# One core: w_in and w_out products of a fused mLSTM cell and gated feed-forward as concurrent 64-row pairs from the third chunk on

## The chip, the cores and the metric

The kernel runs on one core of a Trainium2 chip. A core has a matrix engine (TensorE, PE in the profile, with its weight loads shown as PEld), a vector engine (VectorE, DVE), an activation engine (ScalarE, ACT), a general engine (GpSimd, POOL) and a queue engine (SyncE, SP), which here issues transfers (DMAs). Each engine takes its own instructions in order and waits on semaphores that the others raise. TensorE multiplies a stationary operand that lies on up to 128 rows (partitions) with a moving operand and adds the result up in a bank of PSUM, a memory of eight banks of 128 partitions x 512 float32; VectorE and ScalarE read it from there.

The metric is the device time of one execution in microseconds: the median over runs.

## The reference

Inputs are q, k, v of shape (4, 8, 768, 40), input, forget and output gates, and the weights w_in (320 x 2048) and w_out (2048 x 320). Cut to what matters:

```python
for t in range(S):                                  # mLSTM cell, per batch b and head h
    m_new = np.maximum(f_gate[:, :, t] + m, i_gate[:, :, t])
    f_stab = np.exp(f_gate[:, :, t] + m - m_new)
    i_stab = np.exp(i_gate[:, :, t] - m_new)
    m = m_new
    C = f_stab[:, :, None, None] * C + i_stab[:, :, None, None] * np.einsum('bhd,bhe->bhde', vt, kt)
    n = f_stab[:, :, None] * n + i_stab[:, :, None] * kt
    h_tilde = np.einsum('bhde,bhe->bhd', C, qt)
    denom = np.maximum(np.abs(np.einsum('bhd,bhd->bh', n, qt)[:, :, None]), 1.0)
    y[:, :, t] = sigmoid(o_gate[:, :, t]) * h_tilde / denom
x = y.transpose(0, 2, 1, 3).reshape(3072, 320)      # B*S tokens, H*D features
h = x @ w_in
out = (h * np.cos(h)) @ w_out
```

All of it is float32.

## The kernel before

**Chunks and cells.** The sequence of 768 steps is cut into six chunks of 128 (`NC` = 6). A cell is one chunk of one batch entry, numbered n = c * 4 + b. A cell has within-chunk scores (`scores`, L475: 40 rows, the two heads of a pair on rows 0 to 39 and 64 to 103), decays (`decay_exponents`, `decay`), weighted scores (`weigh`, L481, VectorE), values (`values`, L501 to L510: the tile `vt`, made of pieces of 32 columns of the array), the update of the recurrent state (`seam`, L601: the tile `pu`, 40 columns; `state`, L627, VectorE) and the normalisation (`normalize_turned`, L521 to L538, VectorE), which writes the transposed tokens `xT`, and through `low_out` their last 64 features `xL`.

**The feed-forward.** x has 320 features: `NK` = 2 blocks of 128 rows and a rest of 64. `both_parts(c, b)` takes a chunk's tokens (512 over the four batch entries) through two of eight stages f2 while the cells of the next chunk run. A stage is one `Up`: two tiles `pup` of 128 x 512, one for each block of 128 hidden features, in two PSUM banks (`ps_u`). Each gets two matmuls over 128 rows (L650) and one over 64 rows (L644); the 64-row matmuls of the two tiles use rows 0 to 63 and rows 64 to 127. In even stages and in the last chunk the 64-row pair comes last, in odd ones first. Then ScalarE rounds (`near`, L658), VectorE takes the rest (`rest`, L661), ScalarE takes the sine (`sin`, L666), VectorE multiplies (`gate`, L670). The next stage's `pup` tiles are free once the gates have read them.

**The second product.** From the second chunk on w_out is applied by a scheme with fewer products. `sums` (L719 to L727, VectorE and GpSimd) makes sums and differences S and D of the gated tiles, and `products` gives twelve matmuls of 128 rows and 160 columns per stage (fourteen in the last chunk) into four banks, `acc` = X0, X1, Y0, Y1 (pool `ps_o`, four banks). Sixteen `late_products` per chunk take two more sums into a tile `late` in one bank of the same pool. `combine_first` (L772, ScalarE), `combine` (L780 to L790, VectorE) and `combine_late` (L795 to L797) add the banks up into output tiles, which `out_to` (L696) stores. L760 is the matmul of all these products.

**What sets the order.** It is written out by hand (a manual schedule): each engine gets its instructions in the order of the calls, with semaphores where data pass. `down_slot(c, f2)` says which products are issued at the end of a stage: at f2 = 0 the last twelve of the chunk before, at f2 = 1 the sixteen late ones and then `combine_late`, from f2 = 2 on an even share of this chunk's. `combine` of the chunk before is issued in stage 0, behind the normalisation of that stage's cell. The transfers of q, k, v, decays (`load_E`, tiles E and G), output gates (`load_o`) and the stores are issued on SP where they stand in the code.

The two matmuls of a stage, and the slot of stage 1:

```python
for e, pu in enumerate(self.pu):
    r = slice(64 * e, 64 * e + 64)
    nc.tensor.matmul(pu, w_in_l[r, f2], xL[c][r].rearrange("p b t -> p (b t)"), start=ahead, stop=not ahead)
...
if f2 == 1 and c > 1:
    run(late_products(c - 1), NF)
    combine_late(c - 1)
    return
```

## Time and profile before

| | us |
|---|---|
| median of three runs | 534.6 (534.35 to 534.88) |
| the profiled execution | 531.87, of which the span from the first to the last instruction is 530.1 |
| TensorE busy in the span | 512.8 (97%) |
| VectorE busy | 406.9 (77%) |
| ScalarE busy | 286.6 (54%) |
| GpSimd busy | 247.9 (47%) |

The mean granted clock of TensorE is 0.988. The page gives busy times by engine; a group line names a source line, an engine, the tiles written and read, the shape and how often (x), then busy time and mean duration, then the idle time of the engine ahead of them and what ended it. A float32 matmul shows as two records, two passes. Matmuls overlap, so the time of one is read from start to start, not from its duration. A timeline line has the start and the length in us, the engine, the line, the operation, the tiles and the shape; merged lines are several instructions in a row. SPq is the queue engine's own work, such as issuing a transfer.

Where the chunks lie, by the timeline: the first stage of c = 2 starts at 210.1, of c = 3 at 290.2, of c = 4 at 370.2, of c = 5 at 448.8.

### The profile page before, as it was taken

The page shows a single profiled execution, that of the slowest core. Times are in us where ns is not written, and L with a number is a line of the kernel's source. Part 1 is how long each engine was busy: PE and PEld are TensorE (multiplying, and loading weights), DVE is VectorE, ACT ScalarE, POOL GpSimd, SP SyncE. Part 2 cuts the span into 40 slices and gives each one's busy share as a digit, 9 for nine tenths or more (in the row PEclk, how much of TensorE's full clock was granted, in tenths as well). Part 3 has the DMA queues.
Part 4 walks back from the last instruction along what each step waited for, and adds up shares of the span by engine and source line. Part 5 has one row for each costly group of instructions (what it writes and reads, how often), then busy time and mean ns, then how long its engine had stood idle before and what let it go on. Part 6 is the DMA issues. An engine that isn't in the chain of part 4 may idle for free.

```text
span 530.1 us, 10427 instructions
## 1 busy us (share of the span) xinstructions
PE 512.8 (97%) x3848; PEld 346.9 (65%) x3848; DVE 406.9 (77%) x828; ACT 286.6 (54%) x546; POOL 247.9 (47%) x409
## 2 busy tenths in 40 slices
PE   7999779999999999999999999999999999999996
PEld 3875354556657666676677677677667676666765
DVE  4896798997778878888778888868898878664636
ACT  2896797857556537744547635537735531312221
POOL 7536454673775684554454554453433333121211
PEclk9999879999999999999999999999999999999999
DMA  9999999999339259149159149159110000000001
GB/s 139 227 183 213 231 195 231 246 238 208 48 118 196 56 109 181 41 120 170 56 116 157 42 113 176 49 116 160 47 56 6 1 6 6 26 25 1 1 0 50
DMA packets 97762, 57.81 MB, mean 109 GB/s; under 512 B 62048, under 2 KB 89792, under 8 KB 97712
## 3 DMA queue, kind: packets, MB, share of 16 engines
q1 hardware_dynamic: 96240, 55.64, 51.1%
q0 software_dynamic: 1424, 1.49, 1.4%
q8 instruction: 30, 0.49, 0.4%
q14 instruction: 20, 0.16, 0.1%
q10 hardware_dynamic: 48, 0.02, 0.0%
HBM read 51.71 MB, written 4.11 MB: 105 GB/s over the span
## 4 chain that ended last, share of the span: by engine, by line
PE 81%; DVE 7%; DMA 6%; POOL 1%; issue 1%; SPq 1%; ACT 1%; DVEq 0%; POOLq 0%
PE pup L650 26%; PE acc L760 25%; PE pup L644 8%; PE ps L475 4%; PE po L682 3%; PE late L760 3%; DMA bits<-in_moe_w_in_dram 3%; PE vt L510 2%; PE vt L501 2%; PE pu L601 2%; DMA o<-in_o_gate_dram 1%; PE pw L832 1%; DVE t L456 1%; PE ph L491 1%; DMA bits<-in_moe_w_out_dram 1%
## 5 line engine op out<-in xcount | busy, mean ns | idle before, releaser
L650 PE MATMUL pup<-xT,w_in_sb 128*128 128x512 f32 x384 | 176.7, 603 | 3.1 <-DVE g L670 2.9
L658 ACT ACTIVATE n<-pup 128x512 int32<-128x512 f32 x96 | 54.0, 595 | 193.6 <-PE pup L644 141.6
L650 PEld LDWEIGHTS pup<-xT,w_in_sb 128*128 128x128 f32 x384 | 70.4, 191 | 90.3 <-issue 88.0
L661 DVE SCALAR_TENSOR_TENSOR n<-pup,n 128x512 f32<-128x512 f32 x96 | 63.0, 687 | 82.3 <-ACT n L658 80.9
L724 POOL TENSOR_TENSOR D<-g 128x128 f32<-128x128 f32 x40 | 19.7, 492 | 145.6 <-DVE g L670 145.6
L666 ACT ACTIVATE n<-n 128x512 f32<-128x512 f32 x96 | 59.3, 631 | 16.1 <-DVE n L661 16.1
L670 DVE SCALAR_TENSOR_TENSOR g<-pup,n 128x512 f32<-128x512 f32 x96 | 61.9, 684 | 2.2 <-ACT n L666 1.4
L760 PE MATMUL acc<-w_out_sb,g 128*128 128x160 f32 x320 | 58.6, 304 | 0.0
L760 PE MATMUL acc<-T,g 128*128 128x160 f32 x320 | 58.0, 301 | 0.1
L644 PE MATMUL pup<-xL,w_in_l 64*128 64x512 f32 x192 | 55.2, 650 | 0.9 <-POOL w_in_l L162 0.9
L607 POOL DMA_DIRECT2D xL<-xT x40 | 22.5, 563 | 65.1 <-DVE xT L538 61.6
L760 PEld LDWEIGHTS acc<-w_out_sb,g 128*128 128x128 f32 x320 | 47.8, 190 | 5.6 <-issue 4.2
L760 PEld LDWEIGHTS acc<-T,g 128*128 128x128 f32 x320 | 48.1, 190 | 3.7 <-issue 3.0
L406 ACT ACTIVATE E<-E,tab 128x128 f32<-128x128 f32 x160 | 49.0, 389 | 0.2
L682 PE MATMUL po<-w_out_sb,g 128*128 128x320 f32 x128 | 36.2, 436 | 0.0
L760 PE MATMUL acc<-T,S 128*128 128x160 f32 x160 | 35.0, 300 | 0.0
L475 PEld LDWEIGHTS ps<-t,t 40*128 40x128 f32 (+1 forms) x384 | 24.2, 187 | 12.6 <-DVE t L456 7.5
L682 PEld LDWEIGHTS po<-w_out_sb,g 128*128 128x128 f32 x128 | 24.0, 190 | 11.9 <-issue 1.9
L481 DVE TENSOR_TENSOR E<-ps,E 128x512 f32<-128x512 f32 x48 | 30.7, 680 | 1.4 <-PE ps L475 1.3
L644 PEld LDWEIGHTS pup<-xL,w_in_l 64*128 64x128 f32 x192 | 14.8, 187 | 24.0 <-issue 19.6
L760 PE MATMUL acc<-w_out_sb,S 128*128 128x160 f32 x160 | 28.8, 299 | 0.0
L962 ACT ACT_TABLE_LOAD x22 | 28.2, 1283 | 0.4
(178 smaller groups left out, 878.0 us busy)
## 6 DMA issues: line engine op xcount, KB each, us to landing
E<-M_d SPq DMA_DIRECT2D x22, 512.0 KB, 4.3
qr<-in_q_dram SPq DMA_DIRECT2D x36, 160.0 KB, 3.1
kr<-in_k_dram SPq DMA_DIRECT2D x36, 160.0 KB, 5.4
G<-G_d SPq DMA_DIRECT2D x20, 256.0 KB, 5.2
bits<-in_moe_w_out_dram SPq DMA_DIRECT2D x8, 640.0 KB, 5.8
bits<-in_moe_w_in_dram SPq DMA_DIRECT2D x16, 256.0 KB, 7.6
out_dram<-o_sb SPq DMA_DIRECT2D x24, 160.0 KB, 1.9
ks<-in_k_dram SPq DMA_DIRECT2D x10, 320.0 KB, 7.5
```

What stands on the lines that cost most here:

```text
L406: nc.scalar.activation(out=Es[n][:, h], in_=Es[n][:, h], func=AF.Exp, scale=-1.0, bias=tab[:, c, 0, g:g + 1])
L475: nc.tensor.matmul(ps[j][:, p], kT[r, p], qT[r, p], start=True, stop=True)
L481: nc.vector.tensor_tensor(out=w, in0=pss[n][j], in1=w, op=OP.mult)
L644: nc.tensor.matmul(pu, w_in_l[r, f2], xL[c][r].rearrange("p b t -> p (b t)"), start=ahead, stop=not ahead)
L650: nc.tensor.matmul(pu.rearrange("p (b t) -> p b t", b=B), w_in_sb[:, i, ts(2 * f2 + e, 128)], xT[c][:, i:NK * B:NK], start=(i == 0 and not ...
L658: nc.scalar.activation(out=self.n[e], in_=self.pu[e], func=AF.Copy, bias=0.25)
L661: nc.vector.scalar_tensor_tensor(out=self.n[e].bitcast(FP), in0=self.pu[e], scalar=0.25, in1=self.n[e], op0=OP.add, op1=OP.subtract)
L666: nc.scalar.activation(out=r, in_=r, func=AF.Sin, scale=TWO_PI_DOWN)
L670: nc.vector.scalar_tensor_tensor(out=g, in0=self.pu[e], scalar=TWO_PI, in1=self.n[e].bitcast(FP), op0=OP.mult, op1=OP.mult)
L682: nc.tensor.matmul(po[c][b], gs[c, f][:, ts(b, C)], w_out_sb[:, f], start=(f == 0), stop=(f == NF - 1))
L760: nc.tensor.matmul(a, lhs, rhs, start=start, stop=stop)
L962: nc.scalar.activation(out=spot, in_=spot, func=AF.Sin)
```

## The change

From the third chunk on (c >= 2) every w_in and w_out product is split into its lower and upper 64 rows, and the two halves of different products run as a pair side by side, each writing a bank of its own. `Up.split` takes the two `pup` tiles through five pairs: in the first two, rows 0 to 63 write the second tile and rows 64 to 127 the first; then the tiles are exchanged for three more. `steps` does the same for the w_out products: the upper half runs six products (eight in the last chunk) ahead of the lower, so that the halves are on different banks. `both` issues a pair. When a bank passes from one half to the other, SP waits for the first half's last matmul and signals TensorE (a `nop` on SP), and the first matmul of the other half waits for that signal. Between the two parts of a stage `apart` puts two or three w_out steps, in stage 1 two of the late ones.

The late products have two banks of `ps_o` instead of one. `UPTO` says how many w_out products of a chunk are issued by the end of each stage, in place of equal shares. In the last chunk every third `pup` tile lies in one of the banks of the scores' pool (`thirds`), and that pool's two banks are given out by name (`Banks`). The matmuls of `pu` are cut into 32 and 8 columns in all cells. Half of `state` moves behind the gates of odd stages.

Transfers go through a list: until c = 1 they are issued at once, from c = 2 on up to four are issued between the two parts of each stage and up to two behind `seam`. In the diff, `load_o`, `load_two` and `out_to` change in the same way as `load_E`: `nc.sync.dma_start` becomes `transfer`.

```diff
     dram = ctx.enter_context(tc.tile_pool(name="dram", bufs=1, space=bass.MemoryType.DRAM))
-    ps_a = ctx.enter_context(tc.tile_pool(name="ps_a", bufs=2, space=bass.MemoryType.PSUM))
+    class Banks:
+        def __init__(self, name, tags):
+            self.pool, self.tags, self.turn = ctx.enter_context(tc.tile_pool(name=name, bufs=1, space=bass.MemoryType.PSUM)), tags, 0
+        def tile(self, shape, dtype, name, tag):
+            self.turn = (self.turn + 1) % len(self.tags)
+            return self.pool.tile(shape, dtype, name=name, tag=self.tags[self.turn])
+    ps_a = Banks("ps_a", ("a0", "a1"))
     ps_u = ctx.enter_context(tc.tile_pool(name="ps_u", bufs=2, space=bass.MemoryType.PSUM))
...
+    todo, at_once = [], [True]
+    def transfer(out, in_):
+        todo.append((out, in_))
+        if at_once[0]:
+            issue(len(todo))
+    def issue(n):
+        for _ in range(min(n, len(todo))):
+            dst, src = todo.pop(0)
+            nc.sync.dma_start(out=dst, in_=src)
     def load_o(c, bs=range(B)):
...
-            nc.sync.dma_start(out=E, in_=M_d[1][(c - 1) * BH + b * H:(c - 1) * BH + (b + 1) * H].unsqueeze(0).to_broadcast([128, H, C]))
+            transfer(out=E, in_=M_d[1][(c - 1) * BH + b * H:(c - 1) * BH + (b + 1) * H].unsqueeze(0).to_broadcast([128, H, C]))
...
                     h = 2 * p + j
-                    nc.tensor.matmul(pu[64 * j:64 * j + D, p], kws[n][:, h, 0:D], vs(n)[:, h], start=True, stop=True)
+                    for lo, hi in ((0, 32), (32, D)):
+                        nc.tensor.matmul(pu[64 * j + lo:64 * j + hi, p], kws[n][:, h, lo:hi], vs(n)[:, h], start=True, stop=True)
             pus[n] = pu
...
-    def state(n):
+    def state(n, part=slice(0, 4)):
         if n < N - B:
-            for j, r, s, w in halves(n):
+            for j, r, s, w in list(halves(n))[part]:
                 u = increment(n, r, w)
...
+    SYNC = mybir.DependencyInfo(mybir.DependencyClass.Sync, mybir.DependencyReason.DATA)
+    over = []
+    class Bank:
+        def __init__(self, tile):
+            self.tile, self.half, self.seen = tile, None, None
+    def both(low, high, done):
+        passed = max(bank.seen if bank.half == 1 - half else 0 for half, bank, *_ in (low, high))
+        for half, bank, a, lhs, rhs, start, stop in (low, high):
+            r = slice(64 * half, 64 * half + 64)
+            ins = nc.tensor.matmul(a, lhs[r], rhs[r], start=start, stop=stop).ins
+            if passed:
+                tc.add_manual_dep(ins, over[passed - 1].name, SYNC, reason="a bank passes from one half to the other")
+            bank.half, bank.seen = half, len(over) + 1
+        if done:
+            over.append(nc.sync.nop().ins)
+            tc.add_manual_dep(over[-1], ins.name, SYNC, reason="the halves are done with their banks")
+    thirds = {2 + 6 * i + x for i in range(3) for x in (0, 3)}
+    def third(shape, dtype, name, tag):
+        return ps_a.pool.tile(shape, dtype, name=name, tag=ps_a.tags[spare_bank])
+    spare_bank = 1
     class Up:
...
             self.c, self.f2 = c, f2
-            self.pu = [ps_u.tile([128, B * C], FP, name="pup", tag="up") for _ in range(2)]
+            self.pu = [(third if c == NC - 1 and 2 * f2 + e in thirds else ps_u.tile)([128, B * C], FP, name="pup", tag="up") for e in range(2)]
+            (self.split if c > 1 else self.whole)(c, f2)
+            self.n = [p3.tile([128, B * C], I32, name="n", tag="n") for _ in range(2)]
+        def split(self, c, f2):
+            banks = [Bank(pu) for pu in self.pu]
+            def product(half, e, i, start=False):
+                pu = self.pu[e]
+                if i < NK:
+                    return (half, banks[e], pu.rearrange("p (b t) -> p b t", b=B), w_in_sb[:, i, ts(2 * f2 + e, 128)],
+                            xT[c][:, i:NK * B:NK], start, False)
+                return half, banks[e], pu, w_in_l[:, f2], xL[c].rearrange("p b t -> p (b t)"), False, True
+            for i in range(NK):
+                both(product(0, 1, i, i == 0), product(1, 0, i, i == 0), i == NK - 1)
+            apart(c, f2)
+            issue(4)
+            for i in range(NK + 1):
+                both(product(0, 0, i), product(1, 1, i), False)
+        def whole(self, c, f2):
...
                 low()
-            self.n = [p3.tile([128, B * C], I32, name="n", tag="n") for _ in range(2)]
...
         made = [(X0, 0, G0[:, 0, 0], B11), (X0, 1, G1[:, 0, 0], B21), (X0, 2, S[:, 0], T2),
-                (Y0, 0, G0[:, 0, 1], T3), (Y0, 1, G1[:, 0, 1], T4), (Y0, 2, S[:, 2], T1),
-                (Y1, 2, S[:, 3], B22),
-                (X1, 0, G0[:, 1, 0], B11), (X1, 1, G1[:, 1, 0], B21), (X1, 2, S[:, 1], T2),
-                (Y1, 0, G0[:, 1, 1], T3), (Y1, 1, G1[:, 1, 1], T4)]
+                (Y0, 1, G1[:, 0, 1], T4), (Y0, 0, G0[:, 0, 1], T3), (Y0, 2, S[:, 2], T1)]
         if c == NC - 1:
-            L = late[c]
-            made += [(L, 0, D1, T1), (L, 1, D4, B22)]
-        banks = [id(t) for t, *_ in made]
-        for j, (t, i, lhs, rhs) in enumerate(made):
-            yield t[:, i], lhs, rhs, k == 0 and id(t) not in banks[:j], k == LAST and id(t) not in banks[j + 1:]
+            made += [(late[c], 0, D1, T1), (late[c], 1, D4, B22)]
+        made += [(X1, 0, G0[:, 1, 0], B11), (X1, 1, G1[:, 1, 0], B21), (X1, 2, S[:, 1], T2),
+                 (Y1, 1, G1[:, 1, 1], T4), (Y1, 0, G0[:, 1, 1], T3), (Y1, 2, S[:, 3], B22)]
+        made = [(bank, bank.tile[:, i], lhs, rhs) for bank, i, lhs, rhs in made]
+        if c == 1 and k < LAST:
+            banks = [bank for bank, *_ in made]
+            for j, (_, a, lhs, rhs) in enumerate(made):
+                yield a, lhs, rhs, k == 0 and banks[j] not in banks[:j]
+        else:
+            yield from steps(made, len(made) - 6, k == 0, k == LAST)
+    def steps(made, ahead, first, last):
+        n = len(made)
+        issued = [(half, *made[k]) for j in range(n) for half, k in enumerate((j, (j + ahead) % n))]
+        banks = [m[1] for m in issued]
+        for x in range(0, 2 * n, 2):
+            yield *((*issued[y], first and banks[y] not in banks[:y], last and banks[y] not in banks[y + 1:]) for y in (x, x + 1)), \
+                banks[x:x + 2] != banks[x + 2:x + 4]
     def late_products(c):
-        L = late[c] = ps_o.tile([128, 2, HALF], FP, name="late", tag="o")
-        for k in range(NF // 2):
-            for i, rhs in ((0, wv[:, k, 0, 1]), (1, wv[:, k, 1, 1])):
-                yield L[:, i], Ds[c][:, k, i], rhs, k == 0 and i == 0, k == LAST and i == 1
+        L = late[c] = [Bank(ps_o.tile([128, HALF], FP, name="late", tag="o")) for _ in range(2)]
+        made = [(L[e], L[e].tile, Ds[c][:, k, e], wv[:, k, e, 1]) for e in range(2) for k in range(NF // 2)]
+        return steps(made, NF // 2, True, True)
...
         for _ in range(n):
-            a, lhs, rhs, start, stop = next(made)
-            nc.tensor.matmul(a, lhs, rhs, start=start, stop=stop)
+            now = next(made)
+            if len(now) == 3:
+                both(*now)
+            else:
+                a, lhs, rhs, start = now
+                nc.tensor.matmul(a, lhs, rhs, start=start, stop=False)
     def all_products(c):
-        acc[c] = [ps_o.tile([128, 3, HALF], FP, name="acc", tag="o") for _ in range(4)]
+        acc[c] = [Bank(ps_o.tile([128, 3, HALF], FP, name="acc", tag="o")) for _ in range(4)]
         if c == NC - 1:
-            late[c] = ps_a.tile([128, 2, HALF], FP, name="late", tag="a")
+            late[c] = Bank(ps_a.pool.tile([128, 2, HALF], FP, name="late", tag=ps_a.tags[1 - spare_bank]))
         for k in range(NF // 2):
...
         o = outs_of[c, p] = [out_tile() for _ in range(2)]
-        nc.scalar.copy(out=o[1][:, 0:HALF], in_=acc[c][p][:, 0])
+        nc.scalar.copy(out=o[1][:, 0:HALF], in_=acc[c][p].tile[:, 0])
...
-        X0, X1, Y0, Y1 = acc[c]
+        X0, X1, Y0, Y1 = (bank.tile for bank in acc[c])
         X, Y = (X0, Y0) if p == 0 else (X1, Y1)
...
         o, L = outs_of[c, 1], late[c]
-        tt(out=o[0][:, HALF:DM], in0=L[:, 0], in1=o[0][:, HALF:DM], op=OP.add)
-        tt(out=o[1][:, HALF:DM], in0=L[:, 0], in1=o[1][:, HALF:DM], op=OP.add)
-        tt(out=o[0][:, HALF:DM], in0=L[:, 1], in1=o[0][:, HALF:DM], op=OP.add)
+        L0, L1 = (L.tile[:, 0], L.tile[:, 1]) if c == NC - 1 else (L[0].tile, L[1].tile)
+        tt(out=o[0][:, HALF:DM], in0=L0, in1=o[0][:, HALF:DM], op=OP.add)
+        tt(out=o[1][:, HALF:DM], in0=L0, in1=o[1][:, HALF:DM], op=OP.add)
+        tt(out=o[0][:, HALF:DM], in0=L1, in1=o[0][:, HALF:DM], op=OP.add)
         for e in range(2):
...
-    made_of = {}
+    made_of, late_of = {}, {}
+    done = [0] * NC
+    UPTO = [None, [12 * f2 for f2 in range(8)]] + [[0, 3, 13, 30, 40, 57, 67, 84]] * (NC - 3) + [[0, 3, 19, 35, 51, 67, 83, 98]]
+    def run_to(c, n):
+        if c not in made_of:
+            made_of[c] = all_products(c)
+        run(made_of[c], n - done[c])
+        done[c] = n
+    def apart(c, f2):
+        if f2 == 1 and c > 1:
+            late_of[c - 1] = late_products(c - 1)
+            run(late_of[c - 1], 2)
+        else:
+            d = c if f2 else c - 1
+            run_to(d, done[d] + (2 if c == NC - 1 or f2 % 2 else 3))
...
             else:
-                run(made_of[c - 1], 12)
+                run_to(c - 1, 12 * (LAST + 1))
             return
         if f2 == 1 and c > 1:
-            run(late_products(c - 1), NF)
+            run(late_of[c - 1], LAST - 1)
+            run_to(c, UPTO[c][f2])
+            run(late_of[c - 1], LAST + 1)
             combine_late(c - 1)
             return
-        if c not in made_of:
-            made_of[c] = all_products(c)
-        each = 14 if c == NC - 1 else 12
-        quota = [0] * 8
-        for m in range(2, 8):
-            quota[m] = each * 7 * (m - 1) // 6 - each * 7 * (m - 2) // 6
-        run(made_of[c], each if c == 1 else quota[f2])
+        run_to(c, UPTO[c][f2])
...
                 if cell:
-                    state(n)
+                    state(n, slice(0, 2))
                 for e in range(2):
...
                     up.gate(e)
+                if cell:
+                    state(n, slice(2, 4))
                 if c > 0:
...
                 seam(n)
+                issue(2)
                 normalize_turned(n)
...
         for c in range(NC):
+            at_once[0] = c < 2
             for b in range(B):
                 both_parts(c, b)
-        run(made_of[NC - 1], 14)
+        issue(len(todo))
+        at_once[0] = True
+        run_to(NC - 1, 14 * (LAST + 1))
         for p in range(2):
...
         for p in range(2):
```

More of the change, by code (lines that the diff above doesn't have):

```diff
@@ L309, in load_o @@
                 dst = raw_o[c][32 * a:32 * a + 32].rearrange("t b (g k) d -> t g b (k d)", g=2)[:, g]
-                nc.sync.dma_start(out=dst, in_=src[a, g, c])
+                transfer(out=dst, in_=src[a, g, c])
     def sigmoid(c, bs=slice(0, B)):
@@ L339, in load_two @@
                         dst = raws[name][m][64 * j + 32 * low:64 * j + 32 * low + 32, x:x + WR]
-                        nc.sync.dma_start(out=dst.rearrange("t (p x) -> t p x", x=C // 32 * D),
-                                          in_=src[j, c, :, 4 * b:4 * b + 8])
+                        transfer(out=dst.rearrange("t (p x) -> t p x", x=C // 32 * D), in_=src[j, c, :, 4 * b:4 * b + 8])
         for name, dst, src in (("K", ks2[m], k), ("v", vs2[m], v)):
@@ L344, in load_two @@
                 src = src.rearrange("b h (c t) d -> c t b h d", t=C)
-                nc.sync.dma_start(out=dst[:, :, :, 0:D], in_=src[c, :, b:b + 2])
+                transfer(out=dst[:, :, :, 0:D], in_=src[c, :, b:b + 2])
     def load_E(n):
@@ L360, in load_E @@
             for j in range(2):
-                nc.sync.dma_start(out=G[64 * j:64 * j + 64], in_=src[j, HP * b:HP * b + 2 * HP].unsqueeze(0).to_broadcast([64, 2 * HP, C]))
+                transfer(out=G[64 * j:64 * j + 64], in_=src[j, HP * b:HP * b + 2 * HP].unsqueeze(0).to_broadcast([64, 2 * HP, C]))
             Gs[n], Gs[n + 1] = G[:, 0:HP], G[:, HP:2 * HP]
@@ L695, in out_to @@
     def out_to(c, b, o):
-        nc.sync.dma_start(out=out[b * S + c * C:b * S + (c + 1) * C], in_=o)
+        transfer(out=out[b * S + c * C:b * S + (c + 1) * C], in_=o)
     def weight_sums(part):
```

## The prediction

> **What bounds the kernel now.** I read the page's busy shares first, then the chain that ended last, then the waits, and last the timelines of TensorE, VectorE and SyncE in one chunk. Chunks are numbered c = 0 to 5, as in the code; "stage f2" is one of the eight w_in steps of a chunk.
>
> The page, busy times and the chain's shares:
>
> ```profile
> PE 512.8 (97%) x3848; PEld 346.9 (65%) x3848; DVE 406.9 (77%) x828; ACT 286.6 (54%) x546; POOL 247.9 (47%) x409
> ...
> PE 81%; DVE 7%; DMA 6%; POOL 1%; issue 1%; SPq 1%; ACT 1%; DVEq 0%; POOLq 0%
> ```
>
> TensorE is the bound, and the waits leave it little idle time:
>
> ```profile
> PE pup L650 <- DVE g L670: 2.9, 1, 2.9
> PE vt L501 <- DVE E L481: 2.8, 1, 2.8
> ```
>
> Each is one wait, early in the run. So from c = 2 on only TensorE's own work, and new waits, count. The chain in order of time (start, length, what; a float32 matmul is two records, x8 are four matmuls):
>
> ```profile
> 242.85 3.63 PE pup L650 x8
> 246.48 3.80 PE acc L760 x28
> 250.28 3.43 PE pup L650 x8
> 253.72 1.06 PE pup L644 x4
> 255.67 4.00 PE acc L760 x28
> ```
>
> The same work costs 0.20 us more behind a change of the array's shape: 3.63 against 3.43, 4.00 against 3.80. L644 is the 64-row pair; two pairs of passes at 0.429 (3.43/8) would be 0.86, and 1.06 is again 0.20 more. So a switch costs 0.20, and a 512-column pass costs 0.429 as full rows or as a pair. A 160-column pass costs 3.80/28 = 0.136, a w_out product 0.272.
>
> TensorE's timeline behind the first stage of c = 3 (start, length, line, shapes):
>
> ```profile
> 294.64 1.06 PE L475 MATMUL ps<-t,t 40*128 40x128 f32 x16
> 295.63 0.81 PE L760 MATMUL acc<-w_out_sb,g 128*128 128x160 f32 x4
> ...
> 299.09 0.42 PE L501 MATMUL vt<-E,vs 128*32 128x128 f32 x8
> ...
> 300.75 0.54 PE L601 MATMUL pu<-vs,kw 128*40 128x48 f32 x16
> 301.22 1.13 PE L644 MATMUL pup<-xL,w_in_l 64*128 64x512 f32 x4
> 302.28 3.70 PE L650 MATMUL pup<-xT,w_in_sb 128*128 128x512 f32 x8
> 305.82 4.51 PE L760 MATMUL late<-w_out_sb,D 128*128 128x160 f32 x32
> ```
>
> VectorE in the same stretch:
>
> ```profile
> 300.40 0.28 DVE L722 TENSOR_TENSOR g<-g 128x128 f32<-128x128 f32 x1
> 300.89 0.32 DVE L521 STREAM_TRANSPOSE dt<-vt 128x128 f32<-128x128 f32 x1 [0.21 <-PE vt L510]
> ...
> 303.95 0.48 DVE L780 TENSOR_TENSOR o_sb<-acc,o_sb 128x320 f32<-128x320 f32 x1
> ...
> 305.24 0.31 DVE L784 TENSOR_TENSOR o_sb<-acc,o_sb 128x160 f32<-128x160 f32 x1
> ```
>
> VectorE works through gates, sums, normalisation and the combination of the previous chunk's banks almost without a gap; L784 ends at 305.55, only 0.27 before `late` starts. That near coincidence carries the forecast.
>
> **The change part by part.**
>
> *Switches removed.* A period of two stages with a cell (20.02 us, 241.72 to 261.74) has six shape changes: full to pair, pair to full twice, full to 32 columns (vt), vt to pu, pu to pair. Afterwards two stay, into vt and out of pu. Three at 0.20 go, and vt to pu, 0.14 (0.11 as vt's last step to pu is 0.20 against 0.09 inside vt, and 0.03 in pu's first step). In c = 2 and 3: 8 periods x 0.74. In c = 4 there is no pu: 4 x 0.60 = 2.4. In c = 5 each stage loses two: 8 x 0.40 = 3.2. The number of 512-column slots stays, five per stage.
>
> *pu in 32-column pieces.* 16 records become 32. Bounds: no dearer (its eight steps of 0.042 run four column tiles at once), or 32 x 0.030, vt's mean of 1.66/56, so 0 to 0.6 per cell. Four tiles side by side start 7 ns apart in vt, so I take 0.06. The 8 periods above then give 5.4; the 8 earlier cells in the loop (c = 0 and 1) give 0.08 x 8 = 0.6; the four first cells gain a switch each between px and pu, 0 to 0.8 as TensorE waits there anyway, taken as 0.3. Sum of all this: -11.3.
>
> *The pairs' own pace.* Against 0.136, the scores' pairs cost 0.111 for 128 columns, where streaming as L760 does would give 0.109. So 0 to 0.0024 per pass, on some 950 passes: 0 to 2.3, and 0.5 taken, since the 512-column pairs showed no excess. [...]
>
> *Signals through SP.* 172 wait-and-signal instructions. A matmul's end reaches SP in 0.07 (E's load behind the last vt), VectorE's end reaches TensorE in 0.09; with an SP wait of 0.03 a hand-over takes about 0.2. A 512-column pass ends 0.59 after its start; the other half wants its weights 0.84 after it when two products lie between, so 0.25 of room. For products (end 0.30, use 0.82) it is 0.5. So nothing, as long as SP is free.
>
> *Transfers.* Four issues behind the first half of each stage, two behind pu. At 0.45 to 0.6 each, four take 2 us, and the second half of the stage covers 2.57. The exception, SP's timeline:
>
> ```profile
> 242.78 0.59 SPq L345 DMA_DIRECT2D ks<-in_k_dram  x1
> 243.46 3.83 SPq L345 DMA_DIRECT2D vs<-in_v_dram  x1
> ```
>
> In stage 5 of c = 2 and 3 the batch is G, ks, vs, E. TensorE needs the next signal some 4.1 after the batch begins. SP is through after 2.0 if vs issues freely, and after 7.5 with vs at 4.0 and an E behind it at 2.2 (the one at 78.15). So 0 to 3.4 twice; E and a G leave some 4 us earlier than now, so the backlog before vs is smaller: 0.4 each, 0.8.
>
> *The late products, earlier and in two banks.* Today `late` starts behind a whole stage 1 and takes one bank. Now two of its steps stand between the halves of stage 1, low half and high half in a bank each. By the waits in the changed program these are the banks of X0 and Y0, so TensorE waits for the fourth combination (L784), and the stage's second half, the remaining late products and all that follows queue behind that wait in order. Counted from the end of stage 0 (294.64): VectorE is through after 10.91, less the 0.21 it waited for vt, which now comes sooner; plus 0.09, 10.79. TensorE arrives after scores 0.89, nine products 2.45 (three went between the halves before), switch 0.10, vt 1.55, pu 0.40, switch 0.20 and four passes 1.72: 7.31. It stands 3.5. So in c = 2 too (L784 10.9 behind the stage there); 3.9 in c = 4 without pu. In c = 5 no normalisation precedes: stage 0 ends at 453.31, L784 at 460.73, release 7.51. TensorE needs 2.72 for ten products, waits for the first gate (456.35, so 3.13), and arrives at 4.85: 2.7 plus 0.4. Together 14.0.
>
> *What is late next.* Stage 2 puts products between its halves whose banks the late combination frees: sums and L795 to L797 end about 0.3 behind TensorE's arrival in c = 2 to 4, 0.2 in c = 5: 1.1. With seven instead of fourteen products ahead of vt in even stages, the second weighting (3.3 behind the stage's end, plus 0.1) is 0.1 late, nine times: 0.9. The shorter gaps still cover the gates: 4.9 in even stages against 4.6, 4.07 in odd ones against 3.9 (half of the state update moved behind the gates, and the pair end costs the head start of the first bank). The third bank in c = 5 needs only one gate, 3.13 against 3.80.
>
> **Sum:** -11.3 + 14.0 + 0.5 + 0.8 + 1.1 + 0.9 = +6.0. The profiled execution took 531.87 (span 530.1 and 1.8 around it), which would become 537.9; the median of the runs, 534.6, is 2.7 above it and becomes **540.6**.
>
> **The rivals.**
> - *SP behind vs.* Both batches cost 3.4 instead of 0.4: 546.6. For it: vs at 2.8 to 4.0 in every row. Against: E and two G right ahead of it there.
> - *Faster: the wait doesn't bite.* If the fourth combination were through before TensorE arrives (7.3 behind stage 0, against 10.8 by the rows), the 14.0 go: 526.6. It decides at about 2.0 us of standing per chunk: below that the kernel is faster. Against it: VectorE has only 0.21 of idle time to give.
> - *Hand-overs slower than 0.25.* 0.1 on each of 172 is 17 more: 558. For it: no row shows a signal through SP. Against: each of its legs has a row.
> - *No concurrency.* Pairs one after the other would double TensorE's time from 215 on, some 300 us more: 840. Against: the scores' pairs start 7 ns apart.
> - *Pairs quicker than full rows.* If part of the 0.136 were the load, pairs would come down to the columns' share of a 512-column pass, 0.429 x 160/512 = 0.134: 950 x 0.002 and the 0.5 not spent, 538.2. Against: loads of 190 ns already run under full passes of 0.136. [...]
>
> **How the numbers follow.** Chances: forecast 0.60, SP behind vs 0.15, faster 0.13, slow hand-overs 0.07, no concurrency 0.02, quicker pairs 0.03. Low end 535: all small terms at zero (537.3, without the 3.3), and 2.3 for an error of a sixth in the 14.0. High end 549: pairs at 2.3 and SP at 6.8 add 7.8 to the forecast. The forecast alone spans 535 to 545. 0.2% (1.1 us) is about what a measurement of this kernel can tell from no change. Of the 0.60, 0.05 lie within 1.1 of 534.6 and 0.03 below, so faster 0.16, same 0.05, slower 0.79.
>
> **What would show it.** Right: TensorE idle some 3.5 us ahead of `late` in c = 2 to 4 and 2.7 in c = 5, ended by VectorE; 512-column pairs at 0.43, 160-column ones at 0.136 to 0.139; vt to pu without a step; span near 536. Wrong: no such idle time (faster), idle time ended by SP in stage 5 or at every bank change (slower), or pair steps longer than these.

## The result, and the profile after

The changed kernel is slower: 548.3 us, the median of four runs (545.9 to 551.2), against 534.5 for the kernel before on the same chip (four runs, 532.9 to 534.9). The ratio is 1.0271, 95% interval 1.0236 to 1.0306. The forecast was 540.6 in a range from 535 to 549: the direction was right and the median lies just within the range, but the 6.0 us forecast became 13.8.

The profiled execution after took 550.01 (span 548.2). Its page, busy times and the clock that was granted to TensorE, in tenths, over 40 slices of 13.7 us:

```profile
PE 510.7 (93%) x5376; PEld 377.7 (69%) x5376; DVE 406.8 (74%) x828; ACT 285.2 (52%) x546; POOL 247.5 (45%) x409
...
PEclk9999989999999999899989999989979999999999
```

TensorE is busy about as long as before (512.8) in a span 18.1 us longer. The row of the clock has dips in slices 17, 21, 27 and 30, between 219 and 411 us, where the pairs run. A slice is too coarse to see what they are. First the waits, TensorE from 215 us to its last product (who waited for whom: us in total, times, longest):

```profile
PE late L667 <- DVE o_sb L863: 8.2, 4, 2.5
PE acc L667 <- SPq L672: 3.7, 2, 1.9
PE late L667 <- DVE o_sb L867: 2.4, 4, 0.7
PE acc L667 <- DVE S L790: 0.5, 1, 0.5
```

The kernel before stands 0.3 us in all from c = 2 on; this one stands 15.2 (two waits of 0.2 are left out above). Most of it is the wait that the prediction put into stage 1, in c = 2 on the timeline (start, length, line):

```profile
220.61 1.99 PE L667 MATMUL pup<-xT,w_in_sb 64*128 64x512 f32 x8
...
224.26 0.48 DVE L863 TENSOR_TENSOR o_sb<-acc,o_sb 128x320 f32<-128x320 f32 x1
...
224.80 0.54 PE L667 MATMUL late<-w_out_sb,D 64*128 64x160 f32 x2 [2.20 <-DVE o_sb L863]
...
225.54 0.31 DVE L867 TENSOR_TENSOR o_sb<-acc,o_sb 128x160 f32<-128x160 f32 x1
...
226.00 1.13 PE L667 MATMUL late<-w_out_sb,D 64*128 64x160 f32 x5 [0.67 <-DVE o_sb L867]
```

TensorE is through with the first part of the stage at 222.6, stands 2.20 for the first combination, runs the first late product and stands 0.67 more for the fourth (L784 of the kernel before is L867 here). The other wait is SP's, in stage 5 of c = 2:

```profile
267.46 0.45 SPq L319 DMA_DIRECT2D G<-G_d  x1
267.96 0.74 SPq L319 DMA_DIRECT2D ks<-in_k_dram  x1
268.80 2.01 SPq L319 DMA_DIRECT2D vs<-in_v_dram  x1
...
270.57 0.71 PE L667 MATMUL acc<-T,g 64*128 64x160 f32 x8
271.00 2.32 SPq L319 DMA_DIRECT2D E<-M_d  x1
...
273.42 1.32 PE L667 MATMUL acc<-w_out_sb,g 64*128 64x160 f32 x8 [1.87 <-SPq L672]
...
275.06 1.28 PE L667 MATMUL acc<-T,g 64*128 64x160 f32 x8
```

SP issues vs in 2.0 and the E behind it in 2.3, and the signal that a bank is free stands behind both; c = 3 has the same wait (1.88). The last line shows something that the waits do not: eight products' records that took 0.71 before the stand take 1.28 after it. The trace by stretches of 3.41 us tells why (stretch, length, busy time of PE, PEld, DVE, ACT and POOL with instructions, granted clock, DMA share, GB/s):

```profile
222.39:225.80 3.41, 0.74 (x4) 0.29 (x2) 3.27 (x8) 1.18 (x2) 1.14 (x3) 1.00 0.49 147
225.80:229.21 3.41, 3.21 (x12) 2.86 (x14) 1.43 (x5) 0.00 (x0) 1.29 (x4) 0.50 0.35 124
270.18:273.59 3.41, 1.54 (x24) 1.30 (x22) 2.92 (x7) 2.14 (x4) 2.18 (x7) 1.00 1.43 160
273.59:277.00 3.41, 3.41 (x28) 3.41 (x30) 3.31 (x8) 0.00 (x0) 3.07 (x6) 0.50 0.81 194
307.72:311.13 3.41, 1.58 (x8) 0.39 (x4) 3.20 (x10) 2.53 (x7) 0.94 (x2) 1.00 0.21 54
311.13:314.54 3.41, 2.36 (x15) 2.03 (x17) 2.74 (x8) 0.00 (x0) 2.42 (x6) 1.00 0.93 232
```

In the traces of before and after the granted clock changes on a grid of 3.41 us: within one execution all its changes lie whole multiples of 3.4133 us apart, to 5 ns, over 137 and 138 steps. After a step in which TensorE worked 0.74 or 1.54 us, the whole next step was granted 0.50; after one with 1.58 it was not. Between 215 and 541 us five steps have half the clock: behind the waits of stage 1 in c = 2 (one step) and c = 4 (two), and behind SP's in c = 2 and c = 3. The kernel before has none between 81 and 528. In the half-clock step at 273.59, 160-column passes start 0.267 apart, behind it 0.136; so by estimate a half-clock step in which TensorE works throughout loses half of 3.41, 1.7 us.

The account of the two profiled executions. From the same point (the scores in stage 6 of c = 1, 195.6 before, 195.5 after) to TensorE's last product (524.9, 541.6) the time grew by 16.9. Of that, 15.2 - 0.3 = 14.9 is standing. The five half-clock steps are 17.1 long; TensorE stood for 0.7 of them, and half of the rest, 8.2, is the estimated cost of the clock. So TensorE's own work shrank by 6.2.

| us | forecast | in the trace |
|---|---|---|
| TensorE's own work (switches, pu, the pairs' pace) | -10.8 | -6.2 |
| standing (late, SP, and what is late next) | +16.8 | +14.9 |
| half-clock steps | 0 | +8.2 |
| behind TensorE's last product (5.2 before, 6.5 after) | 0 | +1.3 |
| sum | +6.0 | +18.2 (spans: +18.1; the point of departure lies 0.15 earlier) |

The profiled execution after is one of the slower of its four, that before was 2.7 below its median, hence 18.1 here and 13.8 between medians. The clock is also most of what makes the four runs differ: their spans of 544.1 to 549.4 have mean clocks of 0.986 to 0.975. Without the time that these cost (span times what the clock lacks of 1: 7.6 to 13.7), they are 535.5 to 537.2.

### The profile page after: what moved, and what is told of

Read it like the earlier page. It is cut to its first block, busy times and chain, and to the rows that moved or that the text cites. A ratio compares the mean times of both kernels' runs of the same rounds, so it can differ in the third digit from the quotient of the medians.

```text
span 548.2 us, 13653 instructions
## 1 busy us (share of the span) xinstructions
PE 510.7 (93%) x5376; PEld 377.7 (69%) x5376; DVE 406.8 (74%) x828; ACT 285.2 (52%) x546; POOL 247.5 (45%) x409
## 3 DMA queue, kind: packets, MB, share of 16 engines
q0 software_dynamic: 1424, 1.49, 1.2%
## 5 line engine op out<-in xcount | busy, mean ns | idle before, releaser
L667 PE MATMUL pup<-xT,w_in_sb 64*128 64x512 f32 x512 | 129.9, 607 | 0.2 <-DVE g L740 0.2
L667 PEld LDWEIGHTS pup<-xT,w_in_sb 64*128 64x128 f32 x512 | 60.1, 191 | 24.8 <-issue 20.7
L721 PE MATMUL pup<-xT,w_in_sb 128*128 128x512 f32 x128 | 58.5, 600 | 2.2 <-DVE g L740 2.1
L667 PE MATMUL acc<-w_out_sb,g 64*128 64x160 f32 x528 | 57.0, 303 | 3.7 <-SPq L672 3.7
L667 PEld LDWEIGHTS acc<-w_out_sb,g 64*128 64x128 f32 x528 | 49.6, 192 | 12.1 <-issue 7.5
L667 PE MATMUL acc<-T,g 64*128 64x160 f32 x528 | 55.5, 303 | 0.2 <-DVE g L792 0.2
L667 PEld LDWEIGHTS acc<-T,g 64*128 64x128 f32 x528 | 47.7, 191 | 8.4 <-issue 5.7
L667 PE MATMUL late<-w_out_sb,D 64*128 64x160 f32 x320 | 37.2, 308 | 10.5 <-DVE o_sb L863 8.2
L721 PEld LDWEIGHTS pup<-xT,w_in_sb 128*128 128x128 f32 x128 | 23.3, 190 | 32.3 <-issue 30.9
L667 PEld LDWEIGHTS late<-w_out_sb,D 64*128 64x128 f32 x320 | 33.1, 193 | 15.4 <-DVE o_sb L863 11.5
L667 PE MATMUL acc<-T,S 64*128 64x160 f32 x264 | 35.4, 302 | 0.5 <-DVE S L790 0.5
```

The costliest lines, as they stand in the source:

```text
L667: ins = nc.tensor.matmul(a, lhs[r], rhs[r], start=start, stop=stop).ins
L721: nc.tensor.matmul(pu.rearrange("p (b t) -> p b t", b=B), w_in_sb[:, i, ts(2 * f2 + e, 128)], xT[c][:, i:NK * B:NK], start=(i == 0 and not ...
```

## The experiments

The theory: the pairs themselves save several us; two waits (late products between the parts of stage 1; SP behind vs and E) take that back, and the idle time of both brings half-clock steps on top. The main rival: the pairs draw the lower clock, or are slow in themselves.

**Late products behind stage 1.**

```diff
         if f2 == 1 and c > 1:
-            late_of[c - 1] = late_products(c - 1)
-            run(late_of[c - 1], 2)
+            return
...
-            run(late_of[c - 1], LAST - 1)
+            late_of[c - 1] = late_products(c - 1)
+            run(late_of[c - 1], LAST + 1)
             run_to(c, UPTO[c][f2])
```

> Changed kernel, but in stage 1 of c = 2 to 5 no late products stand between the two parts of the stage; all sixteen follow the stage, the first eight steps ahead of this chunk's first products, as the banks allow. TensorE then reaches the late products about 2.8 us later (2.57 for the second part, 0.25 for a hand-over that nothing covers). Of the 13.7 us that it stood there, some 0.7, 0.7, 1.1 and 0 stay, and the four uncovered hand-overs add 1.0: a gain of about 10.2. Theory (standing still is what halves the granted clock afterwards): the half-clock stretches behind the stalls of c = 2 and c = 4 go too, 3 to 4.5 us more: 533 to 535. Rival (the 64-row pairs themselves draw the lower clock): the stretches stay, somewhere, at the same number: 538 and a mean clock still near 0.980.

Measured: 533.9, ratio to before 1.0003 (0.999 to 1.0016). As the theory had it. The page's row of the clock, and the two largest waits from c = 2 on (1.1 in three others):

```profile
PEclk9999989799999999999999999999999999999998
```

```profile
PE acc L667 <- SPq L672: 2.6, 2, 1.5
PE late L667 <- DVE o_sb L867: 1.0, 3, 0.6
```

No step has half the clock between c = 2 and TensorE's last product, not even behind SP's two waits, which are 1.47 and 1.13 here instead of 1.87.

**vs at the end of its batch.**

```diff
             dst, src = todo.pop(0)
             nc.sync.dma_start(out=dst, in_=src)
+            if not at_once[0] and dst.tensor is vs2[0].tensor or not at_once[0] and dst.tensor is vs2[1].tensor:
+                return
...
-                issue(2)
+                issue(3)
```

> Changed kernel, but a batch of transfers ends behind a load of vs, and three instead of two transfers go behind the state update, so that in stage 5 of c = 2 and 3 the batch is ks and vs alone and the next signal of SP is not behind E's load. Theory: SP is through some 2.8 us after the batch begins, TensorE needs the signal 4.1 after it, the two waits of 1.9 go, and the half-clock stretch that follows each (3.41 us at half speed, 1.7 lost) goes with it: 548.3 - 3.7 - 3.4 = 541. Rival (the clock has nothing to do with the stalls): 544.6, with half-clock stretches still in stage 5 or elsewhere in equal number. Rival (E or vs is needed earlier than it then comes): no gain, with new waits for E or vs.

Measured: 547.4, ratio 1.0263 (1.0247 to 1.028): the 541 were missed. The wait did go (the row of the clock, and the two largest waits from c = 2 on; 0.9 in three others):

```profile
PEclk9999989799999999899999889999999999899998
```

```profile
PE late L669 <- DVE o_sb L865: 8.2, 4, 2.6
PE late L669 <- DVE o_sb L869: 2.4, 4, 0.7
```

SP is no longer among the waits, and the four runs' spans without the clock's part are 530.6 to 533.7, some 4 us below those of the changed kernel. But the mean clock is lower (0.971 to 0.980): in the profiled execution all four stands of stage 1 brought half-clock steps, five together, where only two of the four had brought three before. In c = 3 and c = 5 TensorE stands 2.15 and 1.92 within one step here; in the changed kernel the same stands left at most 1.84 and 1.46 in any step. So 4 us were won by standing less and lost to the clock, as the remaining stands came to lie otherwise on the grid.

**Both edits.**

> Both edits together, late products behind stage 1 and vs at the end of its batch. Theory: 548.3 - 10.2 - 3.7 and no half-clock stretch left between c = 2 and the end, 6 to 8 us more: 526 to 528, mean clock about 0.988 as in the kernel before, and so faster than both kernels by the 11 us that the pairs save less some small waits. Rival (pairs draw the clock, or are slower in themselves): 534 or more, clock near 0.980.

Measured: 529.4, ratio 0.9918 (0.990 to 0.9935). That is 0.8% less than the kernel before, by an interval clear of 1, though 1.4 us above the upper expectation. The page's row of the clock, and the waits from c = 2 on:

```profile
PEclk9999979899999999999999999999999999999999
```

```profile
PE late L669 <- DVE o_sb L869: 1.0, 3, 0.6
PE acc L669 <- DVE S L792: 0.7, 1, 0.7
PE pup L669 <- DVE g L742: 0.2, 1, 0.2
PE acc L669 <- DVE g L794: 0.2, 1, 0.2
```

The half-clock steps of c = 2 to 5 are gone although every product there still is a pair. So pairs alone did not lower the clock here (a mean of 0.986 to 0.992 in six runs, 0.988 to 0.997 in those of the kernel before). (The dips in slices 6 and 8 lie ahead of 106 us, where there are no pairs; the kernel before has such dips in slices 5 and 6.)

**The kernel before, made to stand.** No pairs; the late products in two banks and their first four at the place where the change puts them.

```diff
+            if f2 == 1 and c > 1:
+                late_of[c - 1] = late_products(c - 1)
+                run(late_of[c - 1], 4)
             for i in range(NK):
                 for e, pu in enumerate(self.pu):
```

> Kernel before, without any pairs, but with the late products in two banks and the first four of them put ahead of the 128-row products of stage 1, where TensorE has to wait for the same fourth combination on VectorE. TensorE stands about 3.4, 3.4, 4.0 and 3.7 us there, 14.4 together: 549 if the time is only that of the waits. Theory (standing brings a half-clock stretch of 3.41 us behind it): half-clock stretches appear behind some or all of the four, 1.7 us each: 550 to 556, mean clock below 0.988. Rival (it is the pairs that draw the lower clock): no such stretch after c = 2 begins, 549 and 0.988.

Measured: 553.6, ratio 1.0381 (1.0352 to 1.041).

```profile
PE late L763 <- DVE o_sb L783: 9.5, 4, 2.7
PE late L763 <- DVE o_sb L787: 2.0, 4, 0.7
```

```profile
PEclk9999779999999999799999999999899999799999
```

There are 11.5 us of waits, not the 14.4 expected, and five half-clock steps (two, none, one and two behind the stands of c = 2, 3, 4 and 5). TensorE worked 15.6 us in these, so they cost 7.8: 533.4 + 11.5 + 7.8 = 552.7. Standing cost this kernel without pairs the clock as well (a mean of 0.970 to 0.982 in four runs, 0.988 to 0.997 without the stands). The rival falls.

**w_in in whole rows, w_out in pairs**, on the kernel with both edits (`self.whole(c, f2)` for every chunk, the four transfers behind it).

> The kernel with both edits, but w_in in whole 128-row products again (its 64-row pair stays a pair), w_out still in pairs. Per stage two changes of the array's shape come back, 64 in c = 2 to 5 together. If a change costs 0.20 us, as in the trace of the kernel before, and the pairs' own pace is that of full rows: 64 x 0.20 = 12.8 us more, 529.4 + 12.8 = 542. Rival (what the pairs save does not come from the changes of shape, or the two parts of a stage with hand-overs cost more than a whole one): 529 to 533.

Measured: 536.9, ratio 1.0059 (1.0039 to 1.0078): 7.5 us more than with pairs, between the 12.8 of the theory and the rival's 0 to 4. With the 2.2 of stands that it does not have (0.3 from c = 2 on, against 2.5), the 64 changes of shape cost 9.7, 0.15 each. One stage of it:

```profile
223.82 1.13 PE L719 MATMUL pup<-xL,w_in_l 64*128 64x512 f32 x4
224.88 3.70 PE L725 MATMUL pup<-xT,w_in_sb 128*128 128x512 f32 x8
228.51 2.51 PE L669 MATMUL late<-w_out_sb,D 64*128 64x160 f32 x32
```

From start to start, 223.82 to 228.51, the ten passes take 4.69, and 4.59 in even stages and in c = 5; ten at 0.429 would be 4.29. In the kernel before they take 4.60 in odd stages, 4.49 in even ones and 4.59 in c = 5. As pairs, where nothing waits, they take 4.40 in odd stages, and 4.29 in even ones and in c = 5 (the two parts together). So the pairs bring down the w_in part of a stage by 0.2, in c = 5 by 0.3. The prediction counted on 0.6 for two stages with a cell and on 0.4 for each of c = 5.

**How long a stand must be.** On the kernel with both edits TensorE waits, between the two parts of stages 2 to 7 of c = 2 to 5, for one, three or five small copies on ScalarE in a row that themselves wait for the first part: 24 stands. With five:

```diff
+    def stand():
+        for i in range(5):
+            ins = nc.scalar.copy(out=scratch, in_=scratch).ins
+            if i == 0:
+                tc.add_manual_dep(ins, last_pe[-1].name, SYNC, reason="after the first part")
+        hold.append(ins)
...
             ins = nc.tensor.matmul(a, lhs[r], rhs[r], start=start, stop=stop).ins
+            last_pe.append(ins)
+            if hold:
+                tc.add_manual_dep(ins, hold.pop().name, SYNC, reason="stands")
...
                 both(product(0, 1, i, i == 0), product(1, 0, i, i == 0), i == NK - 1)
+            if f2 > 1:
+                stand()
```

> The kernel with both edits, and between the two parts of stages 2 to 7 of c = 2 to 5 TensorE waits for one small copy on ScalarE that itself waits for the first part: 24 stands of about 0.6 us. Theory (a stand of over 1 us or so makes a half-clock stretch likely, a shorter one doesn't): 24 x 0.6 = 14, no half-clock stretch between c = 2 and the end: 543 to 545. Rival (every stand can bring one): 24 stands with some stretches, 1.7 us each.

> The same with three copies in a row: 24 stands of about 1.5 us, 36 together, 565 without any half-clock stretch. In the four runs so far 1 of 4 stands of 1.1 to 1.9 us outside the batch of transfers brought a stretch. Theory: a stretch behind some 6 to 12 of the 24, 10 to 20 us more: 575 to 585. Rival (stretches have another cause than standing): 565.

> The same with five copies in a row: 24 stands of about 2.4 us, 57 together, 587 without any half-clock stretch. In the runs so far 10 of 12 stands of 1.9 us and more brought a stretch of 3.41 or 6.83. Theory: a stretch behind about 20 of the 24, 34 us or more on top: 620. Rival (another cause): 587.

| copies | stands, us | together | half-clock steps | time |
|---|---|---|---|---|
| 1 | 0.51 to 1.82 | 21.5 | 0 | 556.2 |
| 3 | 1.40 to 2.72 | 43.0 | 1 | 579.7 |
| 5 | 2.31 to 3.61 | 64.9 | 16, in 13 stretches | 625.8 |

With five copies TensorE stood for 3.0 us of the 54.6 in the sixteen steps, so these cost 25.8: 529.4 + 64.9 + 25.8 = 620.1. The rest, 5.7, is 0.24 per stand beyond the gap that the trace shows, as one and three copies have too (0.22 and 0.23); its cause stays open. The sizes were misjudged: in even stages ScalarE is still at the decays, so a stand is 0.9 longer, and three copies brought one step, not 6 to 12. That their 579.7 lies between the expected 575 and 585 is luck. But the rival that standing does not matter to the clock is out: 529.4 + 64.9 = 594 for 625.8. Two pairs of steps with five copies:

```profile
482.10:485.51 3.41, 1.44 (x8) 0.38 (x4) 3.17 (x11) 3.36 (x9) 1.36 (x3) 1.00 0.00 0
485.51:488.92 3.41, 1.76 (x14) 1.23 (x16) 1.16 (x2) 1.50 (x4) 1.11 (x2) 1.00 0.05 19
495.73:499.14 3.41, 1.04 (x10) 0.44 (x8) 2.37 (x3) 2.09 (x5) 1.55 (x2) 1.00 0.00 0
499.14:502.55 3.41, 3.41 (x16) 1.97 (x15) 0.00 (x0) 0.00 (x0) 0.00 (x0) 0.50 0.00 0
```

At 483.5 a stand of 3.61, one of the two longest, is cut in two by the grid, with 1.44 and 1.76 of work in the two steps: no half clock. At 496.3 one of 2.37 lies within one step: half clock.

**Many short stands.** One copy between the parts and four behind the second part, so that the same idle time is spread out.

> The kernel with both edits, and in each of stages 2 to 7 of c = 2 to 5 two shorter stands in place of one long one: one small copy on ScalarE between the two parts of the stage (0.57 us in odd stages, 1.49 in even ones, by the run with one copy) and four copies behind the second part (about 1.9 us in odd stages and in c = 5; in the other even stages the scores' 0.9 lies in it, so 1.0). Some 60 us of standing together, against 68 with five copies in one place; none is longer than 1.9 us, and 3.4 us of work lies between two of them. Theory (what counts is how long TensorE stands within one step of a fixed grid of 3.41 us: below 1.8 us never a half-clock step behind it, from 1.8 to 1.95 in 4 of 14, from 2.15 always): at most two or three half-clock steps, 529.4 + 60 + 0 to 5 = 590 to 594. Rival (it is the standing on average, or the number of stands, that lowers the clock): as many as with five copies, 13 stretches or more, 612 or more.

Measured: 619.1, not 590 to 594. The number is that of the rival, and the expectation was wrong in two sizes. Nine steps had half the clock, not two or three, 15.4 us; and of the 14.6 that remain beyond it and the 59.7 us of gaps, 2.1 are waits of vt for a late weighting; the rest is 0.26 per stand. The nine are no random choice (the last three stretches here lie in c = 3):

```profile
252.48:255.89 3.41, 1.49 (x9) 0.44 (x7) 0.00 (x0) 1.96 (x5) 1.93 (x6) 1.00 1.01 209
255.89:259.30 3.41, 3.41 (x28) 3.41 (x28) 3.15 (x8) 1.90 (x4) 0.24 (x1) 0.50 0.00 0
354.88:358.29 3.41, 1.73 (x10) 0.43 (x6) 0.00 (x0) 1.49 (x4) 2.40 (x6) 1.00 0.96 203
358.29:361.70 3.41, 3.17 (x46) 3.18 (x48) 2.71 (x6) 2.38 (x5) 0.00 (x0) 1.00 0.06 8
382.20:385.61 3.41, 1.51 (x22) 1.52 (x24) 1.05 (x2) 2.96 (x7) 0.67 (x3) 1.00 1.11 132
```

All nine follow a stand of 1.92 that lies whole within one step (1.49 of work). In c = 2 the stands fell so three times in three. In c = 3 the same three stands brought none: two lay across a border of the grid, the third had 1.51 of work in its step and the clock stayed. The nine fit the count by steps, but its border is not one sharp number. Over the profiles of the changed kernel and of the twelve experiments, from 200 us to 6 us ahead of TensorE's last product: of 1204 full-clock steps in which TensorE stood less than 1.80 us none was followed by half the clock; of 24 with 1.80 to 1.95, 13 were; of 21 with 2.15 or more, all; none lies between 1.95 and 2.15. What decides between 1.80 and 1.95 stays open.

**The combination ahead of the normalisation** (c > 1, stage 0), with vs last and the late products where the change puts them.

```diff
                 issue(3)
+                if f2 == 0 and c > 1:
+                    for p in range(2):
+                        combine(c - 1, p)
                 normalize_turned(n)
```

> Changed kernel with the batch of transfers ending behind vs, the late products where the change puts them, between the two parts of stage 1, but the combination of the previous chunk ahead of the normalisation on VectorE. The normalisation takes 2.9 us there, so in c = 2, 3 and 4 the release comes 2.9 us sooner: of the stands of 2.20 + 0.67, 2.20 + 0.67 and 2.54 + 0.3, at most 0.5 each should stay; in c = 5, where no normalisation precedes, 1.2 + 0.7 stays. Theory (it is the order on VectorE that holds TensorE, and stands under 1.8 us leave the clock alone): TensorE's idle time between c = 2 and the end falls from 11.3 to some 4 us, and no half-clock stretch but perhaps one in c = 5: 547.4 - 7 - 5 to 7 = 533 to 535. Rival (normalising later makes a new wait, for vt's bank or for xT): 538 or more.

Measured: 536.3, ratio 1.005 (1.0028 to 1.0072). Most of the way, 11 us less than without it, but 1.3 above the theory's range. The largest waits from c = 2 on (0.9 in three others):

```profile
PE late L669 <- DVE o_sb L869: 3.3, 4, 1.1
PE acc L669 <- DVE o_sb L882: 1.6, 2, 0.8
PE late L669 <- DVE o_sb L865: 1.4, 2, 1.2
```

It is in the main VectorE's order that held TensorE: the stands of stage 1 fall from 10.6 to 4.7. But the rival has a share: the late combination (L882) now comes 0.8 late for the products of stage 2 in c = 2 and 3. The profiled execution, 533.4, has no half-clock step there; it is the fastest of ten.

**The last products in whole rows**, in the order of the kernel before, on the kernel with both edits; then the combination ahead as well.

```diff
+        if c == NC - 1 and k == LAST:
+            made = [made[x] for x in (0, 1, 2, 4, 3, 5, 13, 8, 9, 10, 12, 11, 6, 7)]
...
-        if c == 1 and k < LAST:
+        if c == 1 and k < LAST or c == NC - 1 and k == LAST:
```

> The kernel with both edits, with the last fourteen w_out products of c = 5 as whole 128-row products in the order of the kernel before. Theory (the halves, skewed by eight products, finish their banks late, so that the last combination starts late): of TensorE's 0.66 + 0.18 of standing before the last products about half goes, and the 1.34 us that the time behind TensorE's last product is longer than before go: 529.4 - 1.7 = 527.5. Rival (the longer end has another cause, the combination or the stores): 529 to 530.

> The same and the combination ahead of the normalisation too. Of TensorE's remaining stands, 0.32, 0.33 and 0.66 in stage 1 of c = 2, 3 and 4, the part that VectorE ends goes (0.21, 0.22, 0.56): 1.0 less, 526.5. Rival (the later normalisation makes a new wait): 527.5 or more.

Measured: 528.4, ratio 0.991 (0.9881 to 0.9938), and 533.6, ratio 1.0005 (0.9988 to 1.0022). In the first, the time behind TensorE's last product is 5.2 again, as in the kernel before, but TensorE stands 0.46 + 0.46 for gates and sums there instead of 0.66 + 0.18; the medians differ by 1.0 and the intervals overlap, so a gain over the kernel with both edits is likely and not shown. The second is 5.2 us worse, where 1.0 less was expected. Its largest waits from c = 2 on (1.0 in two others):

```profile
PE acc L669 <- DVE o_sb L884: 2.3, 3, 0.8
PE pup L669 <- DVE g L742: 1.5, 3, 0.8
```

Once the late products stand behind stage 1, an earlier combination has little left to win, and with the normalisation behind it the gates and the late combination come late. TensorE stands 2.6 more than in the first; what makes the rest of the 5.2 is not shown (the profiled executions are 3.2 apart).

## Why the prediction was right or wrong

- *Direction, and the place of the loss: right.* TensorE waits in stage 1 of all four chunks for VectorE's combination, and without that wait the kernel is as fast as before (533.9).
- *The late products' term, 14.0: too high.* The gaps sum to 10.6. In c = 2 the arrival (7.3 behind stage 0, by the trace 222.59 - 215.16 = 7.4) and the release (10.8; 226.00 - 215.16 = 10.8) were right, but one late product, 0.54, runs between the first combination and the fourth, so TensorE stood 2.9 there, not 3.5; c = 4 stood 2.9, not 3.9, and c = 5 1.9, not 3.1.
- *The failed step: the sum had no term for the clock.* It took the standing as time alone. Five half-clock steps behind the stands cost another 8.2 in the profiled execution; that is the largest of the four differences in the account. Without it this execution would be 4.0 above the change forecast, not 12.2. From c = 2 on the trace of before could not speak of it, since TensorE stood no more than 0.16 at a time there. But it shows it earlier, at the two waits of 2.9 and 2.8 that the prediction quoted and passed over (stretches of the kernel before, columns as above):

```profile
57.07:60.48 3.41, 0.57 (x3) 0.07 (x1) 3.34 (x7) 1.51 (x4) 1.79 (x3) 1.00 0.88 231
60.48:63.89 3.41, 3.35 (x4) 1.51 (x5) 2.79 (x6) 2.01 (x3) 1.48 (x2) 0.50 1.01 290
70.72:74.13 3.41, 1.81 (x19) 1.16 (x17) 2.55 (x5) 2.85 (x6) 3.27 (x6) 1.00 1.00 191
74.13:77.54 3.41, 2.22 (x44) 2.23 (x48) 3.34 (x8) 3.12 (x5) 1.36 (x2) 0.50 1.15 188
```

  At 60.48 and at 74.13, each time after a step with much of such a wait, the granted clock is 0.50; whoever looks at the row of the clock beside the row of waits can put a price on a new one.
- *Switches removed, -11.3, with the pairs' pace, +0.5: too large by 4.6.* This is the second step that failed. The price of 0.20 came from the lengths of merged groups, whose ends are modelled; bringing the changes back cost 0.15 each. From start to start the w_in parts fell by 0.2 per stage, 0.3 in c = 5, which is some 3 us short of the forecast in all; where the rest is lost stays open. vt to pu is without a step (0.21), as forecast.
- *Transfers behind vs, 0.8: mis-sized.* It was 3.7, or 1.9 for each batch, between the forecast's 0.4 and the rival's 3.4. The row of before had shown 3.83 for vs. With the smaller backlog vs did come down to 2.0 and 2.2, but the E behind it took another 2.3. With vs last in its batch both waits went.
- *What is late next, 2.0 together: did not come.* No wait for the second weighting or for the late combination is listed from c = 2 to 5. Not foreseen: the halves, skewed by eight products, end the last banks late, so that the time behind the last product is 1.3 us longer, and whole rows there take that back.
- *Signals through SP, 0: right*, apart from 0.1 where nothing lies between the parts of stage 1. *The pairs run side by side* (in stage 5 of c = 2 their starts lie 7 to 10 ns apart, 13 to 14 at half clock), so the rivals of slow hand-overs and of no concurrency are out. Nor are pairs quicker: a 160-column pass takes 0.136 from start to start as a pair too.
- *The faster rival* put the break-even at about 2.0 us of standing per chunk. That is too high, since it rests on the -11.3: with the late products behind stage 1 TensorE stands 5.1 in c = 2 to 5, 1.3 per chunk, with no half-clock step, and the kernel is only as fast as before. With SP's waits gone too it stands 2.5 and is 0.8% faster.
- *The range* held by luck: its high end was made of slower pairs and of SP at 6.8, neither of which came at that size. The profiled execution, 550.0, lies outside it.

## What to carry to other kernels

Price a new wait of an otherwise never idle TensorE at more than its length. In these runs, from 200 us on, half the clock followed 13 of 24 steps of 3.41 us in which TensorE stood 1.80 to 1.95 us, and all 21 with 2.15 or more; for that add half a step (1.7 us, estimated from the granted 0.50), sometimes a whole one (where two such steps came in a row). A shorter stand cost its length and, between the two parts of a stage, some 0.2 more (0.22 with one copy). Before products are moved ahead into a gap, work out when the engine that must free their bank is through, and keep slow transfer issues (2.0 us for vs and 2.3 for E here, with a wait of 1.87) off the queue that passes signals between the halves.

## What the runs showed of the hardware

- In these runs the granted clock changed in steps of 3.41 us. From 200 us on, half the clock followed none of 1204 full-clock steps in which TensorE stood less than 1.80 us, and all 21 with 2.15 or more. Between 60 and 100 us, where much of the rest of a step is small matmuls, it followed 1.4 to 1.6 us in five of the fourteen profiles (among them the kernel before at 70.72, with both edits at 93.1, one copy at 91.3); eight other steps there with 1.4 to 1.7 us brought none, and what decides was not tested. The grid lies differently under the program in each profile (its first border is 0.5 us behind the start of the span in the changed kernel, 2.5 in the kernel before), which fits that one kernel's runs spread over 5 us (545.9 to 551.2), and that removing two stands (vs last) did not remove half-clock steps.
- From 200 us on, in the seven stretches of two half-clock steps TensorE stood 0.38 to 0.98 us in the first of them (0.49 in the changed kernel, at 396.47), in all stretches of one step 0.38 or less.
- In the changed kernel, in stage 5 of c = 2, issuing vs on SP took 2.0 us and the E right behind it 2.3, against 0.45 for a G ahead of them.
